# Linear attention and MLP on one core: four more tiles transposed by VectorE, and a new order of query work around the first MLP block

## The chip, the cores and the metric

The kernel runs on one core of a Trainium2 chip. The core has TensorE (PE, the matrix multiplier; PEld is its loading of the stationary operand), VectorE (DVE), ScalarE (ACT), GpSimd (POOL) and SyncE (SP, which here only issues transfers). A transfer is issued in program order on the queue of the engine that issues it (`SPq`, `ACTq`) and carried by 16 DMA engines. The metric is the device time of one execution in microseconds, lower is better.

## The reference

The input x has 2048 rows of 448 columns. Two layers follow one another with the same weights; all is float32.

```
phi = lambda t: where(t > 0, t + 1, exp(t)) + 1e-6
def A(x):                                   # linear attention, 16 heads of 28
    q, k, v = split_heads(x @ wqkv)
    kv  = sum over rows of phi(k)^T v       # per head, 28 x 28
    z   = sum over rows of phi(k)
    o   = (phi(q) @ kv) / (phi(q) . z + 1e-6)
    return merge_heads(o) @ wo
def B(x):                                   # MLP, 1792 wide
    return gelu_tanh(x @ w1 + b1) @ w2 + b2
for layer in range(2):
    x = x + A(layernorm(x))
    x = x + B(layernorm(x))
```

Note that `phi` needs exp of min(t, 0), plus max(t, 0): the kernel computes max(t, 0) + exp(min(t, 0)) and adds the 1e-6 later.

## The kernel before, in words

**Rows and splits.** The 2048 rows are 16 tiles of 128 rows (t = 0 to 15), four to a block. Every factor of a large product is split into a high and a low half (`XH`, `XL`; `w1h`, `w1l`; `gh`, `gl`), and three products high x high, high x low, low x high are added. ScalarE makes the high half by a cast, VectorE the low half by a subtraction. For a product, TensorE needs a tile with its columns on the partitions, so each normalised tile is transposed.

**Two ways to transpose.** `transpose_x` (line 259) has TensorE do it: four transposes into a PSUM bank `tp`, and `split_x` (273) then casts from `tp` and subtracts. A tile's last 64 columns are doubled ahead of it by a ScalarE copy (in `stage_n` for attention, in `o_n`, line 914, for the MLP). The other way leaves TensorE out: `turn` (298) has VectorE transpose 32 x 32 squares within a tile (two instructions, 384 columns and the tail) into `sq`; two tiles share one such buffer of 1024 columns, 512 KB, and `turn_one` (320) fills a buffer of 512 columns, 256 KB, with one tile. `store_sq` (307) writes it to DRAM on SP's queue, `spread` (312) reads it back with four transfers that put the squares in their places, and `split_t` (327) casts and subtracts from what came back, `sp`.

**Stage one of a layer: keys and the sum G.** `phase1` (697) goes through the tiles in steps t. A step is a string of tokens, `STEPS` (640) or the default `STEP`, and each token issues one piece of work on the engines, in that order: `K` is the key product of tile t (`stage_k`), `kp` its phi, `kh` and `kl` its halves, `X` the split of tile t + 1 (`stage_x`, 466), `T` its transposes by TensorE if it takes the first way (`stage_b`, 459), `s` the split of the normalised rows (`stage_s`), `a`, `n` and `v` or `tu` statistics, normalising and turning of later tiles (`stage_a`, `stage_n`, `stage_t`, 448), `sp` the spreads of all that is stored (`stage_sp`), `ld` loads of x, `G` the product of the keys of tile t - 1 with the normalised rows, added up over all tiles, `Q` the query product, `qp` the phi of queries. `bg` loads and splits a piece of the MLP's weights in layer 0 (ScalarE and GpSimd). An odd tile's turn also stores its pair. `TURNED = (8, 0)` (433) says from which tile on a layer takes VectorE's way: tile 8 in layer 0, all tiles in layer 1.

`k_at`, `q_at` and `g_at` (484 and below) give the places of the low products among the eleven matmuls of a product: a later place gives the low half more time.

**From stage one to the MLP.** The string `ORDER` (631) is the same kind of list for what lies between: the last G, the small matrices made of G, then for the first block of four tiles the attention output (`o`), its statistics (`la`, `o_ln`, line 896), normalising (`lb`), turning (`tu`, `turn_xm`, line 928), storing (`st`), spreading (`sp`, transfers in turn on SP's and ScalarE's queue) and splitting (`x`, `m_split`, line 935). Tiles 0 and 1 share a buffer, tile 2 has its own, and tile 3 is transposed by TensorE (`T3`, `m_transpose`, line 924). The query products of tiles 9 to 15 stand between these tokens (`Q`, `Qx`, `Qy`, `Qa`), so that TensorE has work while the block's tiles are got ready. A query's phi is two tokens: `Qi` (`phi_first`, line 576) is two ScalarE passes, Relu of -q and Exp of minus that, and `Qj` (`phi_last`, line 583) is VectorE's max(q, 0) plus that, and its store. Tokens take the queries in the order of their products.

**The MLP.** `mlp1` (961) is the product with a piece of w1, `hp` (its first one takes all high halves of the block first), then GELU on ScalarE, the cast to `gh` on ScalarE and the subtraction to `gl` on VectorE. `mlp2` (981) is the product with w2, added over 14 pieces into `y`. The next block's attention output and splits are issued between these pieces.

**What sets the order.** Nothing is planned by a program: every engine and every queue runs its instructions in the order in which the tokens issue them, and an instruction waits until what it reads is there and its buffer is free. Buffers come from named pools with a few buffers each (tags `"A"`, `"B"`, `"S"`, `"e"`, `"E"`).

## Time and profile before

| | before |
|---|---|
| median of 3 runs (lowest to highest) | 866.67 us (866.61 to 866.70) |
| the profiled execution | 866.77 us |
| its span in the profile | 865.0 us |
| TensorE busy | 859.5 us, 99% |
| VectorE busy | 489.9 us, 57% |
| ScalarE busy | 354.0 us, 41% |
| GpSimd busy | 209.1 us, 24% |

The span runs from the first to the last instruction that the profiler recorded; 1.77 us of the execution lie around it. In the span, layer 0's key products end at 96.8 us, the MLP of its first block begins at 135 us, and layer 1's key products begin at 436 us.

How to read the rows: a row of the timeline has the start, the time (both in us), the engine, the line of the kernel, the operation, the tile written and the tiles read (`psk<-wk,XL`), the shape and the number of instructions that it merges; in brackets stands an idle time before it and what ended it. In a merged row the time is that from its first to its last instruction. A matmul's own duration includes its pipeline, so two starts tell more of its cost than its duration. A row of the waits has who waited, for whom, the total, the number and the mean, in us. `ACTq` and `SPq` are transfers being issued. In a row of the transfers, the last two numbers are the size of one transfer and its time from issue to landing in us.

### The profile page before, as it was taken

To read this page: it belongs to the slowest core of one execution; us is meant where nothing else is said; L and a number is where in the kernel's file an instruction comes from. 1 tells how busy PE (TensorE), PEld (TensorE's weight loads), DVE (VectorE), ACT (ScalarE), POOL (GpSimd) and SP (SyncE) were. 2 spreads that over 40 slices of the span, in tenths; PEclk is the share of its full clock that TensorE was granted. 3 is DMA by queue.
4 is the path that set the end of the run, shared out by engine and by line. 5 is a ranking of instruction groups with operands and counts; after the bars stand their busy time and mean duration, and the time that the engine had idled before them with its cause. 6 is when DMAs were issued, how large, how long until landed. Compare 5 with 4: busy or idle time off the path is not lost.

```text
span 865.0 us, 11671 instructions
## 1 busy us (share of the span) xinstructions
PE 859.5 (99%) x4173; PEld 769.9 (89%) x4173; DVE 489.9 (57%) x956; ACT 354.0 (41%) x634; POOL 209.1 (24%) x242
## 2 busy tenths in 40 slices
PE   9999999999999999999999999999999999999998
PEld 8999988888888888888899998988888888888887
DVE  7888676559455443236477877664674383533112
ACT  6776656333323322333356565632232233223231
POOL 3565612235013012012222343120220140140000
PEclk9999999999999999999999999999999999999999
DMA  5475546633313502051145543362332423111001
GB/s 168 131 241 178 187 112 206 194 112 109 135 60 114 150 0 98 1 182 49 49 149 187 164 129 97 108 217 81 116 107 91 135 74 114 50 49 42 1 1 43
DMA packets 65082, 95.81 MB, mean 111 GB/s; under 512 B 9088, under 2 KB 59904, under 8 KB 65024
## 3 DMA queue, kind: packets, MB, share of 16 engines
q1 hardware_dynamic: 63696, 94.13, 33.8%
q10 hardware_dynamic: 1328, 0.93, 0.4%
q8 instruction: 33, 0.54, 0.3%
q14 instruction: 25, 0.20, 0.1%
HBM read 56.70 MB, written 35.13 MB: 106 GB/s over the span
## 4 chain that ended last, share of the span: by engine, by line
PE 95%; ACT 2%; DMA 1%; DVE 1%; issue 0%; POOL 0%; ACTq 0%; SPq 0%; DVEq 0%
PE hp L972 31%; PE y L1002 10%; PE y L1001 10%; PE y L1003 10%; PE G L622 8%; PE psk L353 8%; PE psq L353 5%; PE op L891 2%; PE op L890 2%; PE op L892 2%; DMA sp<-sq_m 1%; PE op L880 1%; PE op L879 1%; PE op L881 1%; PE kvp L786 1%; PE mp L796 1%
## 5 line engine op out<-in xcount | busy, mean ns | idle before, releaser
L978 DVE TENSOR_TENSOR gl<-g,gh 128x512 fp32r<-128x512 f32 x112 | 83.2, 743 | 293.2 <-ACT gh L977 293.2
L974 ACT ACTIVATE g<-hp,b1s 128x512 f32<-128x512 f32 x112 | 77.1, 688 | 400.1 <-PE hp L972 400.1
L1002 PE MATMUL y<-w2l,gh 128*128 128x448 f32 x447 | 163.6, 366 | 0.0
L1001 PE MATMUL y<-w2h,gh 128*128 128x448 f32 x447 | 162.2, 363 | 0.0
L1003 PE MATMUL y<-w2h,gl 128*128 128x448 f32 x447 | 160.3, 359 | 0.1
L972 PE MATMUL hp<-XH,w1h 128*128 128x512 f32 x336 | 130.7, 389 | 0.0
L972 PE MATMUL hp<-XH,w1l 128*128 128x512 f32 x336 | 130.7, 389 | 0.0
L972 PE MATMUL hp<-XL,w1h 128*128 128x512 f32 x336 | 130.1, 389 | 0.0
L215 POOL TENSOR_TENSOR brs<-bve,mhalf 128x1 f32<-128x1 f32 x55 | 34.8, 632 | 258.4 <-DVE bve L214 257.9
L1001 PEld LDWEIGHTS y<-w2h,gh 128*128 128x128 f32 x447 | 83.7, 187 | 9.8 <-ACT gh L977 0.5
L1002 PEld LDWEIGHTS y<-w2l,gh 128*128 128x128 f32 x447 | 83.9, 188 | 6.9
L1003 PEld LDWEIGHTS y<-w2h,gl 128*128 128x128 f32 x447 | 84.0, 188 | 5.8 <-DVE gl L978 0.9
L972 PEld LDWEIGHTS hp<-XL,w1h 128*128 128x128 f32 x336 | 63.1, 188 | 13.1
L972 PEld LDWEIGHTS hp<-XH,w1h 128*128 128x128 f32 x336 | 63.0, 187 | 10.7
L972 PEld LDWEIGHTS hp<-XH,w1l 128*128 128x128 f32 x336 | 63.1, 188 | 9.9
L977 ACT CAST gh<-g 128x512 fp32r<-128x512 f32 x112 | 69.6, 622 | 3.6
L840 POOL TENSOR_TENSOR pz<-pq,zb 128x448 f32<-128x448 f32 x32 | 37.0, 1162 | 103.3 <-DVE dn L846 67.1
L353 PE MATMUL psk<-wk,XH 128*128 128x448 f32 x210 | 61.8, 364 | 0.0
L353 PE MATMUL psq<-wq,XH 128*128 128x448 f32 x196 | 57.5, 366 | 0.0
L478 POOL TENSOR_TENSOR xnl<-x,xnh 128x384 fp32r<-128x384 f32 x32 | 35.0, 1092 | 69.3 <-ACT xnh L477 56.0
L622 PE MATMUL G<-kh,xnh 128*128 128x448 f32 x128 | 46.8, 368 | 0.0
L336 DVE TENSOR_TENSOR XL<-sp,XH 128x512 fp32r<-128x512 f32 x54 | 45.3, 851 | 2.1 <-ACT XH L335 2.1
(185 smaller groups left out, 1491.1 us busy)
## 6 DMA issues: line engine op xcount, KB each, us to landing
x<-in_A_x_dram SPq DMA_DIRECT2D x32, 224.0 KB, 3.7
pq_d<-eq SPq DMA_DIRECT2D x32, 224.0 KB, 2.7
pq<-pq_d SPq DMA_DIRECT2D x32, 224.0 KB, 3.1
sq_m<-sq SPq DMA_DIRECT2D x14, 512.0 KB, 2.6
x<-x_d SPq DMA_DIRECT2D x32, 224.0 KB, 3.7
sp<-sq_m SPq DMA_DIRECT2D x52, 128.0 KB, 2.8
sq_a<-sq SPq DMA_DIRECT2D x12, 512.0 KB, 2.9
sp<-sq_a SPq DMA_DIRECT2D x48, 128.0 KB, 2.7
```

The source lines that it names most:

```text
L336: eng.tensor_tensor(lo.rearrange("p (c i n) -> p c i n", c=4, n=32), x, f(h), op=OP.subtract)
L353: pe.matmul(o, x, p, start=(i == 0), stop=(i == 10))
L478: pool.tensor_tensor(lo[:, :TL], xn[:, :TL], f(h[:, :TL]), op=OP.subtract)
L622: pe.matmul(acc[c], w, k, start=first and c not in others[0], stop=last and c not in others[1])
L840: pool.tensor_tensor(pz, pqt[l, b * 4 + j], tr.zb, op=OP.mult)
L972: pe.matmul(o, w, r, start=(k == 0), stop=(k == len(made) - 1))
L974: act.activation(g, hp, AF.Gelu_apprx_tanh, bias=b1s[:, i:i + 1])
L977: act.copy(gh, g)
L978: dve.tensor_sub(gl, g, f(gh))
L1001: pe.matmul(acc[j], gh[:, s], w2h[:, i], start=first, stop=False)
L1002: pe.matmul(acc[j], gh[:, s], w2l[:, i], start=False, stop=False)
L1003: pe.matmul(acc[j], gl[:, s], w2h[:, i], start=False, stop=stop)
```

## The change

Five things are changed together:

- In layer 0, tiles 6 and 7 take VectorE's way too (`TURNED` becomes 6). The steps 3 to 11 of layer 0 are written anew: each pair of tiles is turned, stored and spread in other steps than before, and the last pair, tiles 14 and 15, later. The three functions that place the low products follow.
- In most of these steps the split of the next tile (`X`) is issued ahead of the keys' phi (`kp`).
- In both layers the fourth tile of the MLP's first block is turned by VectorE instead of TensorE: `tu3`, `st2` and `sp2` stand where `T3` stood, and its split, `x3`, now comes last of the four.
- For the queries of tiles 12, 13 and 14 the first step of phi is min(q, 0) by VectorE (`Qm`) and one Exp by ScalarE (`Qe`), instead of two passes by ScalarE.
- The two buffers of one tile, for tile 2 and tile 3, come from different pools ("A" and "B").

```diff
--- before.py
+++ after.py
@@ -311,14 +311,14 @@
 
     def spread(key, h, queues=(sp,)):
         d = stored.pop((key, h))
-        r = spreads[key, h] = half("sp") if d.shape[1] == 1024 else t512("A", 2, "sp")
+        r = spreads[key, h] = half("sp") if d.shape[1] == 1024 else t512("AB"[h - 1], 2, "sp")
         d = d.rearrange("(i r) (m f) -> m r i f", i=4, m=4)
         for m in range(4):
             eng = queues[m % len(queues)]
             eng.dma_start(r[m * 32:(m + 1) * 32].rearrange("r (i f) -> r i f", i=4), d[m])
 
-    def turn_one(x, key):
-        sq = squares[key, 1] = t512("A", 2, "sq")
+    def turn_one(x, key, h):
+        sq = squares[key, h] = t512("AB"[h - 1], 2, "sq")
         sq = sq.rearrange("p (m c n) -> p c m n", m=4, c=4, n=32)
         dve.transpose(sq[:, :3], x[:, :TL].rearrange("p (c m n) -> p c m n", c=3, n=32))
         dve.transpose(sq[:, 3].rearrange("p (u m) n -> p u m n", u=2),
@@ -326,7 +326,7 @@
 
     def split_t(key, t, hi, lo, eng=dve):
 
-        x = spreads[key, t // 2]
+        x = spreads[key, t - 1 if (key, 2) in spreads and t == 3 else t // 2]
         if x.shape[1] == 512:
             x = x.rearrange("p (i c n) -> p c i n", i=4, c=4)
         else:
@@ -430,7 +430,7 @@
     sts = {}
 
 
-    TURNED = (8, 0)
+    TURNED = (6, 0)
     tails = {}
 
     def stage_a(l, t):
@@ -483,18 +483,18 @@
 
     def k_at(l, t):
         if t < 9:
-            return (3, 6, 9, 11) if t == 0 or l == 0 and 2 < t < 8 else (2, 5, 8, 11)
+            return (3, 6, 9, 11) if t == 0 or l == 0 and 2 < t < 6 else (2, 5, 8, 11)
         return (2, 5, 8, 11) if t == 9 else (1, 4, 7, 10)
 
     def q_at(l, t):
         if t < 9:
-            return (2, 5, 8, 11) if l == 0 and t < 7 else (2, 4, 7, 10) if t == 0 else (1, 4, 7, 10)
+            return (2, 5, 8, 11) if l == 0 and t < 5 else (2, 4, 7, 10) if t == 0 else (1, 4, 7, 10)
         return {11: (4, 7, 10, 11), 12: (5, 7, 9, 11),
                 13: (5, 8, 10, 11), 15: (1, 5, 8, 11)}.get(t, (1, 4, 7, 10))
 
     def g_at(l, t):
         if t < 9:
-            return (4, 7, 10) if l == 0 and 0 < t < 6 else (3, 6, 9)
+            return (4, 7, 10) if l == 0 and 0 < t < 4 else (3, 6, 9)
         return (2, 5, 8) if t < NT - 1 else (2, 6, 9)
 
     def stage_k(l, t, cs=range(4)):
@@ -579,6 +579,16 @@
         act.activation(e, o, AF.Relu, scale=-1.0)
         act.activation(e, e, AF.Exp, scale=-1.0)
         begun.append((l, t, o, e))
+
+    def phi_min():
+        l, t, o = qo.pop(0)
+        e = t512("e" if t < NT - 2 else "E", 3 if t < NT - 2 else 2, "eq")[:, :D]
+        dve.tensor_scalar(e, o, 0.0, None, op0=OP.min)
+        begun.append((l, t, o, e))
+
+    def phi_exp():
+        e = begun[-1][3]
+        act.activation(e, e, AF.Exp)
 
     def phi_last():
         l, t, o, e = begun.pop(0)
@@ -631,8 +641,8 @@
     ORDER = [
         "Q ld1 ld0 ld2 G qz1 qz0 qz2 gt qs1 Q Qp kv qs0 tq1 Qx mask tq0 qs2 ld3 b "
         "m0 qh1 ql1 m1 ms0 qh0 ql0 m2 ms1 m3 ms2 tq2 ms3 Qi qz3 o0 qh2 qs3 la0 ql2 Qj o1 tq3 qh3 la1 ql3 "
-        "o2 lb0 tu0 la2 o3 lb1 tu1 st0 la3 lb2 tu2 st1 Qy Q lb3 T3 sp0 sp1 Qi Qa x3 Qj x0 x1 x2 Qi Qj pre "
-        "Qa Qi Qj Qa Qi Qj Qi Qj "
+        "o2 lb0 tu0 la2 o3 lb1 tu1 st0 la3 lb2 tu2 st1 Qy Q Qi lb3 tu3 sp0 st2 Qm sp1 Qe Qa sp2 Qj Qj "
+        "Qm Qe Qj x0 x1 x2 pre Qa Qm Qe x3 Qa Qi Qj Qj "
     ] * LAYERS
     DEFER = NT - sum(tok in ("Q", "Qa", "Qy") for tok in ORDER[0].split())
 
@@ -640,12 +650,15 @@
     STEPS = {
         (0, 1): "T X a3 q1 s kh n3 kl q1 G bg ld",
         (0, 2): "K T X s a4 kp n4 a5 kh kl n5 a6 G bg Q ld",
-        (0, 3): "qp K T X s a7 kp kh n6 kl a8 G bg Q ld",
-        (0, 4): "qp K T X s a9 kp kh n7 n8 kl n9 v8 v9 G bg Q ld sp",
-        (0, 8): "qp K T X s a kp n kh kl tu a14 G bg Q ld sp",
-        (0, 9): "qp K T X s kp n14 kh kl v14 G bg",
-        (0, 10): "K T X s a15 kp n15 kh kl v15 G bg sp",
-        (0, 11): "K T X kp s kh kl G bg",
+        (0, 3): "qp K T X n6 s a7 kp kh n7 kl v6 v7 G bg Q ld sp",
+        (0, 4): "qp K T X s a8 kp kh n8 a9 kl v8 n9 G bg Q ld",
+        (0, 5): "qp K s X kp kh v9 a10 kl n10 G bg Q ld sp",
+        (0, 6): "qp K s X v10 kp kh a11 kl n11 G bg Q ld",
+        (0, 7): "qp K s X kp v11 kh a12 kl n12 G bg Q ld sp",
+        (0, 8): "qp K s X kp v12 kh a13 kl n13 a14 G bg Q ld",
+        (0, 9): "qp K X s v13 kp n14 kh kl G sp bg",
+        (0, 10): "K X s v14 kp a15 kh kl n15 G bg",
+        (0, 11): "K X v15 kp s kh kl G sp bg",
         (1, 0): "K T X s kp kh kl a n tu Q ld sp",
     }
     NORM = (
@@ -914,30 +927,17 @@
     def o_n(l, b, j):
         t = b * 4 + j
         xn = xns["m", l, t] = ln_norm(sts.pop(("m", l, t)), f"xm{l}_{t}", OP.add if b == 0 else OP.subtract)
-        if b == 0 and j == 3:
-            act.copy(xn[:, D:], xn[:, TL:D])
 
     def add_bias(l, b, j):
         t = b * 4 + j
         pool.tensor_tensor(xt[l, t], xt[l, t], b2b, op=OP.add)
-
-    def m_transpose(l, b, j):
-        xn = xns.pop(("m", l, b * 4 + j))
-        transpose_x(xn, xn[:, TL:], ("m", l, b), j)
 
     def turn_xm(l, j):
         xn = xns.pop(("m", l, j))
         if j < 2:
             turn(xn, ("m", l, 0), j)
         else:
-            turn_one(xn, ("m", l, 0))
-
-    def m_split(l, b, j):
-
-        if j < 3:
-            split_t(("m", l, b), j, *block(("m", l, b)).pieces(j))
-        else:
-            split_x(("m", l, b), j)
+            turn_one(xn, ("m", l, 0), j - 1)
 
 
     def q_prep(l, b, j, tr):
@@ -1133,15 +1133,14 @@
 
         tok_ = SimpleNamespace(
             Q=lambda j: stage_q(l, fill.pop(0)), Qp=lambda j: fill_qphi(), Qv=lambda j: stage_qphi(j or 9),
-            Qi=lambda j: phi_first(), Qj=lambda j: phi_last(), Qx=lambda j: stage_q(l, fill[0], (0,)),
+            Qi=lambda j: phi_first(), Qm=lambda j: phi_min(), Qe=lambda j: phi_exp(), Qj=lambda j: phi_last(), Qx=lambda j: stage_q(l, fill[0], (0,)),
             Qy=lambda j: stage_q(l, fill.pop(0), (1, 2, 3)),
             Qa=lambda j: stage_q(l, fill.pop(0), tag="acc"), G=lambda j: stage_g(l, NT - 1, acc, lambda: trans_z(tr, zs[l])),
             ld=lambda j: (load_pq(l, 0, j), load_x(l, j)), gt=lambda j: trans_gt(tr, acc),
             kv=lambda j: trans_kv(tr), mask=lambda j: trans_mask(tr), m=lambda j: trans_m(tr, j),
             ms=lambda j: trans_ms(tr, j), qz=lambda j: q_z(l, 0, j, tr), qs=lambda j: q_scale(l, 0, j, tr),
             tq=lambda j: q_transpose(l, 0, j), qh=lambda j: q_high(l, 0, j), ql=lambda j: q_low(l, 0, j), o=lambda j: o_mm(l, 0, j, tr),
-            la=lambda j: o_ln(l, 0, j), lb=lambda j: o_n(l, 0, j), T=lambda j: m_transpose(l, 0, j),
-            x=lambda j: m_split(l, 0, j), tu=lambda j: turn_xm(l, j),
+            la=lambda j: o_ln(l, 0, j), lb=lambda j: o_n(l, 0, j), x=lambda j: m_part(l, 0, j), tu=lambda j: turn_xm(l, j),
             st=lambda j: store_sq(("m", l, 0), j), sp=lambda j: spread(("m", l, 0), j, (sp, act)), pre=pre, b=biases)
         for tok in ORDER[l].split():
             name, j = tok.rstrip("0123456789"), int("0" + tok.lstrip("abcdefghijklmnopqrstuvwxyzQTG"))
```

## The prediction

> **What bounds the kernel now.** I read the page first (busy shares), then the list of waits, then the timeline at the places that the change touches.
>
> ```profile
> span 865.0 us, 11671 instructions
> PE 859.5 (99%) x4173; PEld 769.9 (89%) x4173; DVE 489.9 (57%) x956; ACT 354.0 (41%) x634; POOL 209.1 (24%) x242
> ...
> PE warm L170 <- DVE one L164: 1.1, 1, 1.1
> PE psk L567 <- ACT wk L137: 0.8, 1, 0.8
> ```
>
> TensorE is busy for 99% of the span and waits, as the profile shows it, for 1.9 us. So a matmul taken out of its stream is time won, unless the work put in its place makes TensorE wait; and there is nearly no wait that a faster ScalarE could shorten. The rest is about those two things.
>
> **The change part by part.**
>
> *Transposes taken from TensorE.* These rows are its stream around tile 6's transposes (first four) and around those of the MLP block's fourth tile (last four):
>
> ```profile
> 42.61 0.37 PE L353 MATMUL psk<-wk,XL 128*128 128x448 f32 x1
> 42.81 0.49 PE L264 MATMUL tp<-ident,x 128*128 128x128 f32 x3
> 43.14 0.27 PE L264 MATMUL tp<-ident,b2b 128*128 128x128 f32 x1
> ...
> 43.46 0.36 PE L622 MATMUL G<-kl,xnh 128*128 128x448 f32 x1
> ...
> 127.71 0.37 PE L353 MATMUL psq<-wq,XL 128*128 128x448 f32 x1
> 127.92 0.60 PE L264 MATMUL tp<-ident,xm 128*128 128x128 f32 x4
> 128.28 1.06 PE L353 MATMUL psq<-wq,XH 128*128 128x448 f32 x4
> 129.17 0.36 PE L353 MATMUL psq<-wq,XL 128*128 128x448 f32 x1
> ```
>
> From 42.61 to 43.46 are 0.85 us with two ordinary matmuls in them, which start 0.20 us apart elsewhere: four transposes cost 0.45 us. From 127.71 to 129.17 are 1.46 us with five matmuls: 0.46 us. There are four such groups (tiles 6 and 7, and the fourth tile in each of two layers): 4 x 0.45 = **-1.8 us**. The ScalarE copies that go (two tails in the first stage, the 64-column copy per layer) stood beside waits and are worth nothing.
>
> *The fourth tile's new way.* Before, its transposed copy was split ahead of the others while the other three tiles' DMA round trip ran. After, the tile itself makes that trip: two transposes on VectorE, a 256 KB store on SP, four 64 KB reads on SP and ScalarE's queue, then the cast on ScalarE. The first matmul of the MLP reads the high halves of all four tiles, so it cannot start before that cast. Its cover is the three query tiles (13 to 15) that TensorE works on; it used up:
>
> ```profile
> 125.33 0.58 DVE L323 STREAM_TRANSPOSE sq<-xm 128x384 f32<-128x384 f32 x1
> 125.83 0.27 DVE L324 STREAM_TRANSPOSE sq<-xm 128x128 f32<-128x128 f32 x1
> 126.95 0.51 DVE L227 TENSOR_SCALAR xm<-x,bst,brs 128x448 f32<-128x448 f32 x1 [0.85 <-POOL brs L908]
> ...
> 127.56 1.77 ACTq L318 DMA_DIRECT2D sp<-sq_m  x4
> ...
> 131.37 1.66 ACT L335 CAST XH<-sp 128x512 fp32r<-128x512 f32 x3 [0.36 <-DMA sp<-sq_m]
> 131.64 0.61 DVE L585 SCALAR_TENSOR_TENSOR eq<-psq,eq 128x448 f32<-128x448 f32 x1
> 132.18 1.89 DVE L336 TENSOR_TENSOR XL<-sp,XH 128x512 fp32r<-128x512 f32 x3
> ...
> 127.92 3.29 DMA sp<-sq_m
> ...
> 136.63 0.58 ACT L580 ACTIVATE eq<-eq 128x448 f32<-128x448 f32 x1
> 139.98 0.69 DVE L978 TENSOR_TENSOR gl<-g,gh 128x512 fp32r<-128x512 f32 x1 [2.12 <-ACT gh L977]
> ...
> 135.01 0.39 PE L972 MATMUL hp<-XH,w1h 128*128 128x512 f32 x1
> 140.00 0.47 PE L1001 MATMUL y<-w2h,gh 128*128 128x448 f32 x1
> 140.31 0.37 PE L1002 MATMUL y<-w2l,gh 128*128 128x448 f32 x1
> 140.73 0.47 PE L1003 MATMUL y<-w2h,gl 128*128 128x448 f32 x1
> 141.04 0.36 PE L1001 MATMUL y<-w2h,gh 128*128 128x448 f32 x1
> ```
>
> I follow it in the times of this profile. The tile is normalised at 127.47; its two transposes take 0.77 us as tile 2's do (125.33 to 126.10): 128.25. The store goes out on SP at 128.3, ahead of the second spread there. A 256 KB store alone and the transfers issued at that moment took
>
> ```profile
> sq_m<-sq SPq DMA_DIRECT2D x1, 256.0 KB, 2.2
> ...
> sp<-sq_m ACTq DMA_DIRECT2D x2, 64.0 KB, 3.3
> ```
>
> so it lands between 130.5 and 131.6. I take 131.6, as the 16 DMA engines are full then (four spreads of 128 KB are under way, and the row at 127.92 took 3.29 us). ScalarE's queue must now issue its two reads of it, in order ahead of the next exponentials: the first waits for the store, the second also for the first spread's last transfer, whose semaphore it reuses (landed at 131.21). At 0.44 us an issue (1.77 / 4) ScalarE is free at 131.65 at the earliest, 132.7 at the latest, and I take **132.2**.
>
> From there ScalarE and VectorE take turns, in the order that the program has. Exponential of tile 13's query to 132.8; VectorE's last pass of it (0.54 to the next row) to 133.35; three low halves (0.60 each; the high halves run ahead of them) to 135.15; then VectorE's new min(q, 0) of tile 14's query, for which no row exists: the nearest, a one-input pass over 448 columns at 0.51 and a pass reading the same PSUM tile at 0.61, bound it, and I take 0.55 to 135.7. The exponential behind it waits for that min, and the fourth tile's cast stands behind the exponential: 0.49 to the cast's start, 0.62 for the cast: 136.9. TensorE wants to start at 135.01 - 0.45 = 134.56, so **it waits 2.35 us** in each layer (1.8 to 2.9 from the ends above). The min saves ScalarE a pass of about the exponential's length for each of three queries, but puts VectorE's queue, with three low halves in it, ahead of the cast.
>
> A part of this comes back. Before, TensorE's first y matmuls wait for the first gh and gl: their starts stand 0.31, 0.42 and 0.31 us apart instead of 0.20, so 0.44 us are lost, because ScalarE has four query exponentials and the table load still to do. After, one query is left behind the cast: its exponential starts some 0.6 us after the cast, and from the last exponential to the end of the first gl are 4.04 us (136.63 to 140.67): 4.6 us, while TensorE gets there only 4.99 us after the cast (135.01 to 140.00). So -0.44. With the transposes' 0.45 a layer pays 2.35 - 0.45 - 0.44 = +1.46 us. Layer 1 has the same rows 425.3 us later.
>
> *Tiles 6 and 7 in the first stage.* Each pair now needs a store and a spread, and all later pairs are stored one step later (13 in step 9, 15 in step 11). Two places are tight, tile 6's trip and the last pair's:
>
> ```profile
> 34.50 0.61 DVE L533 TENSOR_TENSOR za<-psk,za 128x448 f32<-128x448 f32 x1
> 50.51 0.36 PE L622 MATMUL G<-kl,xnh 128*128 128x448 f32 x1
> ...
> 80.08 0.32 SPq L310 DMA_DIRECT2D sq_a<-sq  x1
> 87.37 0.62 ACT L335 CAST XH<-sp 128x512 fp32r<-128x512 f32 x1 [0.88 <-DMA sp<-sq_a]
> 88.02 0.69 DVE L336 TENSOR_TENSOR XL<-sp,XH 128x512 fp32r<-128x512 f32 x1 [0.79 <-ACT XH L335]
> 89.97 0.37 PE L353 MATMUL psk<-wk,XL 128*128 128x448 f32 x1
> ```
>
> Store to cast is 7.3 us, and tile 14's cast already waits 0.88 us for it; the low half is done at 88.71, 1.26 us before TensorE reads it. After, TensorE is 0.9 us earlier there, and tile 15 is turned only behind the low half of tile 12, whose own trip began at about 71.5: 71.5 + 7.3 + 0.62 + 0.69 + 0.7 = 80.75 instead of 80.05. So the slack of 1.26 becomes 1.26 - 0.9 - 0.7 = -0.3 us. Tile 6: its pair is turned behind the row at 34.50 (0.4 us later than there, then 2 x 0.77), so stored at 37.0; with three loads between store and spread on SP the trip takes nearer 8 us, and the cast, at 45, now stands ahead of key 5's exponentials. Cast 0.6, two exponentials 1.1, the keys' pass 0.6, one tile's transposes 0.8, statistics 0.9 and kl 0.6 end at 49.6, just when TensorE, 0.9 earlier than 50.51, reads kl. I put **+0.4 us** on both together; between 0 (if VectorE is a little ahead) and 1.4 (if both trips are 0.5 us longer).
>
> Here a rule bears on the size:
>
> ```profile
> 63.25 0.69 DVE L336 TENSOR_TENSOR XL<-sp,XH 128x512 fp32r<-128x512 f32 x1
> 69.91 1.50 DVE L336 TENSOR_TENSOR XL<-sp,XH 128x512 fp32r<-128x512 f32 x1
> 69.70 1.15 POOL L404 TENSOR_TENSOR w1x<-stg,w1x 64x448 fp32r<-64x448 f32 x1
> ```
>
> A low half made from a spread takes 0.69 us, or 1.50 us while GpSimd works; tiles 6 and 7 now are of this kind. I count 0.69, because GpSimd's split of tile 5 should be over when tile 6 gets there. The Trainium skill (SBUF — State Buffer, "Who interferes with whom") says that a VectorE instruction with two SBUF inputs and a GpSimd instruction that reads SBUF exclude each other; the row agrees (+0.8 us), and by it the sum would be up to 0.8 us higher if they met.
>
> The shifted positions of low products, the splits ahead of the keys' phi, and the earlier loads of the next queries have a microsecond or more of cover each in the queues of ScalarE, VectorE and SP, and I count nothing for them.
>
> **The sum.** Transposes -1.8, waits for the fourth tile 2 x 2.35 = +4.7, y's waits 2 x -0.44 = -0.9, first stage +0.4: **+2.4 us**. The profiled execution took 866.77 us (span 865.0 and 1.77 around it), 0.1 above the median of 866.67, so I forecast **869.1 us**. Its own ends: per layer +0.9 to +2.0, first stage 0 to +1.4 with its two groups' -0.9: 867.6 to 871.2.
>
> **The rivals.**
> *The cover holds (faster).* If the fourth tile's cast is done by 134.5, in both layers, TensorE never waits for it, all 1.8 us stay, and y's waits go too: 866.67 - 1.8 - 0.9 = 864.0, with nothing lost in the first stage. For it: the query work covers 6.3 us from 128.25. Against: store and spread alone take 2.2 + 2.8 us, and the orders on ScalarE and VectorE put a min, an exponential and three splits between. It decides where the wait is under 1.14 us a layer: 2 x (1.14 - 0.89) = 0.5 = 0.9 - 0.4, and the kernel is not slower.
> *Only the trip counts (same).* If ScalarE's issue does not block as I think, the cast follows the landing, at 134.6 and 0.6 on: a wait of 0.7 us a layer, 2 x (0.7 - 0.89) - 0.9 + 0.4 = -0.9: 865.8.
> *TensorE's clock falls.* The granted clock is full in all slices of the page, but the first products run at half speed:
>
> ```profile
> PEclk9999999999999999999999999999999999999999
> ...
> 1.12 4.21 PE L170 MATMUL warm<-one 128*128 128x128 f32 x18 [1.12 <-DVE one L164]
> ```
>
> 18 products in 4.0 us are 0.22 us each, against 0.11 for the transposes at 42.81. If a pause of 2.35 us threw the clock back, 4.0 us at half speed would lose 2 us a layer: 869.1 + 4 = 873.1. No pause of this length is in the trace. The Trainium skill (TensorE: Matmul & The Clock Gate, Part 1) has the clock halve after an idle window of about 3.4 us, free-running; by it 2.35 us would hardly do, and no run here shows it.
>
> **How the numbers follow.** Forecast 0.74, cover holds 0.05, only the trip 0.13, clock 0.08. A 0.2% step is 1.7 us (864.9, 868.4), about what a measurement tells from none. The forecast's own spread puts 0.56 above 868.4 and 0.18 between. Slower: 0.56 + 0.08 = 0.64; same: 0.18 + 0.13 = 0.31; faster: 0.05. Leaving out cover, trip's lower part and clock, the range is 866.4 to 871.2.
>
> **What would show it.** After: no transposes from tile 6 on; a TensorE wait of about 2.4 us for XH ahead of the first hp in both layers, with ScalarE's cast last in order behind min and exponential; y's first matmuls 0.20 apart; a few tenths at the keys of tile 14. Wrong, if that wait is under 1 us, if the store lands before 130.7, or if keys of tiles 12 to 15 wait over a microsecond.

## The result, and the profile after

The changed kernel takes **875.8 us** (median of four, 874.75 to 876.81) against 866.68 us: a ratio of 1.0104 (95% interval 1.009 to 1.0117). It is 9.1 us slower. I had forecast +2.4 us and a range that ended at 871.2.

The page of the profiled execution (875.2 us, span 873.4 us), and under it the waits in which TensorE takes part (who waited, for whom: total, times, longest, in us):

```profile
span 873.4 us, 11687 instructions
PE 860.3 (99%) x4157; PEld 768.8 (88%) x4157; DVE 496.8 (57%) x970; ACT 349.7 (40%) x624; POOL 210.7 (24%) x242
...
PE hp L972 <- ACT XH L335: 5.9, 2, 3.0
PE psk L353 <- DVE XL L336: 1.5, 2, 0.9
...
PE G L632 <- DVE kl L526: 0.5, 1, 0.5
```

TensorE has 16 instructions fewer, as meant, and is busy for *more* time. Three kinds of wait of 0.5 us and more that did not exist before stand here. They sum to 7.9 us, less than the 8.4 by which the span grew, though 1.8 us of transposes went out of it. So some of the time is elsewhere. The starts of landmark matmuls in the two traces tell where (us; each difference is that of the stage between two landmarks):

| from | to | before | after | difference |
|---|---|---|---|---|
| start of the span | first key product | 7.07 | 6.58 | -0.5 |
| first key product | first matmul on G's blocks (stage one of layer 0) | 98.77 | 101.21 | +2.4 |
| there | first hp, layer 0 | 29.17 | 31.91 | +2.7 |
| there | first key product of layer 1 (MLP) | 301.03 | 302.34 | +1.3 |
| there | first matmul on G's blocks, layer 1 | 95.13 | 95.13 | 0.0 |
| there | first hp, layer 1 | 29.17 | 31.76 | +2.6 |
| there | end | 304.70 | 304.46 | -0.2 |

The sum is +8.3. It is made up of the two transitions, stage one, and something in the MLP of layer 0 that layer 1 does not have. That last is seen in TensorE's timeline around the first hp of both layers:

```profile
136.31 0.36 PE L353 MATMUL psq<-wq,XL 128*128 128x448 f32 x1
139.69 0.49 PE L972 MATMUL hp<-XH,w1h 128*128 128x512 f32 x1 [3.03 <-ACT XH L335]
140.03 0.39 PE L972 MATMUL hp<-XH,w1l 128*128 128x512 f32 x1
140.26 0.40 PE L972 MATMUL hp<-XH,w1h 128*128 128x512 f32 x1
...
143.01 0.63 PE L972 MATMUL hp<-XL,w1x 128*128 128x512 f32 x1
143.44 0.63 PE L972 MATMUL hp<-XH,w1h 128*128 128x512 f32 x1
143.87 0.63 PE L972 MATMUL hp<-XH,w1l 128*128 128x512 f32 x1
...
565.71 0.36 PE L353 MATMUL psq<-wq,XL 128*128 128x448 f32 x1
568.92 0.50 PE L972 MATMUL hp<-XH,w1h 128*128 128x512 f32 x1 [2.85 <-ACT XH L335]
```

An ordinary query matmul is followed by the next 0.20 us later; here hp follows after 3.38 and 3.21 us, so TensorE loses **3.18 and 3.01 us** ahead of the first hp. Then hp's matmuls stand 0.23 us apart (140.03 to 140.26), and from 141 us on 0.43 us apart (143.01 to 143.44). The table of stretches shows why. A row has the stretch, its length, the busy time of PE, PEld, DVE, ACT and POOL, the granted TensorE clock (1.00 is full), the busy share of the DMA engines and GB/s:

```profile
136.50:139.70 3.20, 0.17 (x2) 0.01 (x1) 2.05 (x5) 1.72 (x5) 0.00 (x0) 1.00 0.96 324
139.70:141.00 1.30, 1.30 (x6) 1.09 (x7) 1.30 (x3) 1.25 (x3) 1.29 (x1) 1.00 0.85 167
141.00:144.30 3.30, 3.30 (x10) 2.52 (x9) 0.43 (x1) 1.82 (x3) 0.39 (x1) 0.50 0.96 339
144.30:148.00 3.70, 3.70 (x18) 3.24 (x17) 0.69 (x1) 2.00 (x4) 0.00 (x0) 0.98 0.75 251
```

For 3.3 us the clock is granted at 0.50: 1.7 us lost. It falls 1.3 us *after* TensorE has gone on. In layer 1 of this execution it does not fall at all. The mean granted clocks of the four executions are 0.998, 0.995, 0.996 and 0.997, and one such interval is 3.4 x 0.5 / 873 = 0.002 of the mean: one to two or so of them in each.

Why hp waits is on ScalarE, VectorE and in the chain of waits. The rows below are the spread's issues on ScalarE's queue with the exponentials (L591) and casts (L335) behind them, VectorE's rows of the same time, and the chain's piece for the fourth tile's store:

```profile
134.06 0.85 ACTq L318 DMA_DIRECT2D sp<-sq_m  x2
134.95 0.58 ACT L591 ACTIVATE eq<-eq 128x448 f32<-128x448 f32 x1 [3.38 <-DMA sq_m<-sq]
135.44 1.64 ACT L335 CAST XH<-sp 128x512 fp32r<-128x512 f32 x3
138.56 0.58 ACT L591 ACTIVATE eq<-eq 128x448 f32<-128x448 f32 x1 [1.48 <-DVE eq L586]
139.04 0.60 ACT L335 CAST XH<-sp 128x512 fp32r<-128x512 f32 x1
...
136.10 1.89 DVE L336 TENSOR_TENSOR XL<-sp,XH 128x512 fp32r<-128x512 f32 x3
137.91 0.62 DVE L586 TENSOR_SCALAR eq<-psq 128x448 f32<-128x448 f32 x1
...
130.22 3.75 DMA sq_m<-sq
```

ScalarE stands idle for 3.38 us for the fourth tile's store. Then comes the order that the forecast described, piece for piece: exponential, casts and low halves, the min at 137.91 behind them, ScalarE's 1.48 us of waiting for it, the exponential, the cast, hp.

In stage one TensorE stalls at three places, ahead of the low key half of tile 5 and ahead of the low halves of tiles 10 and 14:

```profile
49.10 0.36 PE L632 MATMUL G<-kh,xnh 128*128 128x448 f32 x1
49.99 0.47 PE L632 MATMUL G<-kl,xnh 128*128 128x448 f32 x1 [0.52 <-DVE kl L526]
...
71.70 0.37 PE L632 MATMUL G<-kl,xnh 128*128 128x448 f32 x1
72.93 0.47 PE L353 MATMUL psk<-wk,XL 128*128 128x448 f32 x1 [0.87 <-DVE XL L336]
...
90.80 0.36 PE L632 MATMUL G<-kl,xnh 128*128 128x448 f32 x1
91.79 0.47 PE L353 MATMUL psk<-wk,XL 128*128 128x448 f32 x1 [0.62 <-DVE XL L336]
```

By their starts, less 0.20 each: 0.7, 1.0 and 0.8 us. The chain of waits from 45 to 92 us is one ring that goes round four times (start, time, what):

```profile
57.55 0.63 ACT XH L335
...
58.21 1.54 DVE XL L336
...
60.29 0.47 DVE sq L303
...
60.98 3.19 DMA sq_a<-sq
...
65.56 5.87 DMA sp<-sq_a
...
71.53 0.63 ACT XH L335
...
72.88 0.49 DVE sq L303
...
73.58 2.58 DMA sq_a<-sq
...
77.50 3.01 DMA sp<-sq_a
```

The split of tile 8 (57.55), behind it on VectorE the turn of tile 11 (60.29), the pair's store (60.98) and spread, the split of tile 10 (71.53), behind it the turn of tile 13, its store and spread, and so on to tile 14 at 90.39. A pair is turned only after the split that waited for the pair before it. Before, pairs were stored every 12 us (at 55.86, 68.11 and 80.08), which is TensorE's pace; a round of the ring takes 14.0 us (57.55 to 71.53) where the spread is slow. Before, tile 10's spread had landed 5.5 us ahead of its cast (63.71 and 69.24). Now its pair is stored 5.1 us later, and from the store to the last landing are 10.4 us, not 7.9, so that this slack is gone; why that spread is the slowest of the five is not shown.

### The profile page after: what moved, and what is told of

Same layout as the page of the kernel before. It is cut to its first block, busy times and chain, and to the rows that moved or that the text cites. A ratio compares the mean times of both kernels' runs of the same rounds, so it can differ in the third digit from the quotient of the medians.

```text
span 873.4 us, 11687 instructions
## 1 busy us (share of the span) xinstructions
PE 860.3 (99%) x4157; PEld 768.8 (88%) x4157; DVE 496.8 (57%) x970; ACT 349.7 (40%) x624; POOL 210.7 (24%) x242
## 4 chain that ended last, share of the span: by engine, by line
PE 87%; DMA 6%; DVE 3%; ACT 1%; issue 1%; SPq 1%; POOL 1%; DVEq 0%; ACTq 0%; POOLq 0%
PE hp L972 32%; PE y L1002 10%; PE y L1001 10%; PE y L1003 10%; PE G L632 5%; PE psk L353 5%; PE psq L353 3%; DMA sp<-sq_a 2%; PE op L904 2%; DMA sq_a<-sq 2%; PE op L903 2%; PE op L905 2%; DMA sq_m<-sq 1%; SPq L318 1%; PE op L893 1%
## 5 line engine op out<-in xcount | busy, mean ns | idle before, releaser
L336 DVE TENSOR_TENSOR XL<-sp,XH 128x512 fp32r<-128x512 f32 x58 | 48.4, 846 | 9.5 <-ACT XH L335 9.5
L632 PE MATMUL G<-kl,xnh 128*128 128x448 f32 x128 | 46.2, 366 | 0.5 <-DVE kl L526 0.5
```

The source lines that it names most:

```text
L336: eng.tensor_tensor(lo.rearrange("p (c i n) -> p c i n", c=4, n=32), x, f(h), op=OP.subtract)
L632: pe.matmul(acc[c], w, k, start=first and c not in others[0], stop=last and c not in others[1])
```

## The experiments

All of them compute the whole result. Waits are given by the starts of matmuls, less 0.20 us, as above.

**The two halves of the change, each alone.** First, everything behind stage one as changed, with `TURNED`, `STEPS` and the low products' places as before:

```diff
-    TURNED = (6, 0)
+    TURNED = (8, 0)
...
 (STEPS, k_at, q_at and g_at as before the change)
```

> Layer 0's stage one as before (transposes of tiles 6 and 7 by TensorE, the old steps), all that comes after it as changed. Theory (now, from the trace after the change): the fourth tile's trip makes TensorE wait 3.2 us ahead of the first hp in each layer, +0.1 behind it, -0.45 for the transposes, -0.44 for y's waits: 2 x 2.4 = +4.8 us, 871.5 us; and each such pause can throw TensorE's clock to half speed for some microseconds, which costs another 0 to 4 us and differs between executions (spread over 1 us). Rival (the forecast's own sum): 2 x 1.46 = +2.9 us, 869.6 us, with the clock at 1.000 and the runs within 0.3 us of each other.

Measured: 872.95 us (872.43 to 874.78), ratio 1.0078 (1.0061 to 1.0094). The waits ahead of hp are 2.97 and 2.90 us. Half-speed matmuls follow in layer 0 of the profiled execution and not in layer 1; the four granted clocks are 0.998, 0.995, 1.000 and 0.997, and the spans follow them: 870.8, 873.1, 870.0 and 870.9 us. The forecast's own sum (869.6) does not hold; the transition alone is the greater part of the loss, and the part that differs between executions goes with the clock.

Second, stage one alone (the new `STEPS`, `TURNED = (6, 0)`, the old `ORDER`):

> Tiles 6 and 7 by VectorE with the new steps of layer 0's stage one; all that comes after as before. Theory: three stalls of TensorE in stage one (0.8 at the keys of tile 5, 1.1 at tile 12's split, 0.9 at tile 14's, 0.3 of small ones) less 0.9 for eight transposes: +2.2 us, 868.9 us. The clock stays at 1.000 and the runs lie within 0.3 us, since no pause is over 1.3 us. Rival (the forecast): +0.4 - 0.9 = -0.5, 866.2 us. Rival for the clock: if it fell for another reason than the pause, it falls here too.

Measured: 869.35 us (868.78 to 870.19), ratio 1.0032 (1.0019 to 1.0045). Stalls of 0.8, 0.6 and 1.3 us at the three places, and the granted clock 0.999 to 1.000 in every execution: pauses of up to 1.3 us leave it alone. (What the expectation calls tile 12's split is tile 10's: the pair stored at 61 us is tiles 10 and 11.) The two parts sum to 6.3 + 2.7 = 9.0 us, the whole to 9.1: as far as executions that differ by 2 us can tell, they do not help or hinder each other.

**The order ahead of the fourth tile's cast.**

```diff
-        "Qm Qe Qj x0 x1 x2 pre Qa Qm Qe x3 Qa Qi Qj Qj "
+        "Qm Qe Qj x0 x1 x2 pre Qa x3 Qm Qe Qa Qi Qj Qj "
```

> The changed kernel with the fourth tile's split issued ahead of tile 14's min and exponential. Theory (the order on ScalarE and VectorE costs what the trip does not): the cast starts right behind the three others, so the wait ahead of the first hp falls from 3.2 to about 1.2 us in each layer, and the clock does not fall; but the two last queries' exponentials then lie between it and the first GELU, so y waits 0.5 to 1.0 us a layer. Sum against the changed kernel without its lost clock (873.5): -4.0 + 1.0 to 2.0: 870.5 to 871.5 us, runs within 0.3 us. Rival (only the landing of the tile counts): the wait stays above 2.5 us, and the time at 873 or above.

Measured: 870.87 us (869.79 to 873.71), ratio 1.0055 (1.0034 to 1.0075). The waits ahead of hp fall to 1.4 and 0.8 us, and no half-speed matmul follows. As expected, part of it comes back ahead of y: 0.8 us, and 0.4 more among its first matmuls, in each layer. The last expectation failed: executions differ by 3.9 us at a clock of 0.999 to 1.000. The profiled one (the slowest) waits 1.2 us at 47 us, in stage one, where the changed kernel's trace has no wait: two of the four spreads of tiles 6 and 7 landed at 47.0 and 47.6 us, where all had landed by 45.4 in the changed kernel's trace, and the other two came at 44.4 and 44.7. The cast waited for them:

```profile
46.99 0.36 PE L353 MATMUL psq<-wq,XH 128*128 128x448 f32 x1
48.40 0.47 PE L353 MATMUL psk<-wk,XH 128*128 128x448 f32 x1 [1.05 <-ACT XH L335]
```

So the new stage one has places without slack, where a late transfer moves the total. That the other executions differ for the same reason is not shown, as they were not profiled.

**The min, undone.** The queries' first step by two ScalarE passes (`Qi`) again, nothing else:

```diff
-  ... sp0 st2 Qm sp1 Qe Qa sp2 Qj Qj Qm Qe Qj x0 x1 x2 pre Qa Qm Qe x3 ...
+  ... sp0 st2 sp1 Qi Qa sp2 Qj Qj Qi Qj x0 x1 x2 pre Qa Qi x3 ...
```

> The changed kernel with the queries' exponentials made by two passes of ScalarE as before, instead of VectorE's min and one pass. If the min behind the three low halves is what holds the fourth tile's cast, ScalarE goes on from its third cast at once: two passes for tile 14 (1.1 us) in place of waiting 1.5 us and one pass (0.5), but one pass more for tile 13 (0.55): the wait ahead of hp falls by 0.2 to 0.4 us a layer. If ScalarE's load were the bound, it would rise by 0.5 to 1.1.

Measured, in one execution: 875.03 us. The waits are 2.77 and 2.50 us instead of 3.18 and 3.01: 0.4 and 0.5 us less, a little over what was expected. One pass *more* on ScalarE for each of three queries makes the wait *shorter*. Behind both pauses the clock fell (granted mean 0.995), so that nothing of it is seen in the time.

**ScalarE's queue freed of the wait for the store.** From the kernel with the transition alone changed, the fourth tile's four reads all go out on SP:

```diff
- spread(("m", l, 0), j, (sp, act))
+ spread(("m", l, 0), j, (sp,) if j == 2 else (sp, act))
```

> As the run with the transition alone changed, but the four reads of the fourth tile go out on SP's queue alone, so that ScalarE has no issue to wait for. Theory (ScalarE stands 3.4 us behind an issue that waits for the store, and everything behind it is late): tile 13's exponential and the three casts run some 2 us earlier, the fourth tile's cast follows its landing (0.6 us later than there, four issues in a row on SP), and the wait ahead of the first hp falls from 2.9 to between 1.3 and 1.8 us a layer; 869.1 + 1.77 - 2 x 1.3 = 868.3 us, without a fall of the clock. Rival (only the landing counts): the wait does not fall, since the landing is later: 871 us or more.

Measured: 868.19 us (867.65 to 869.85, ten executions), ratio 1.0019 (1.001 to 1.0029), 4.8 us less than the 872.95 without this line. The waits are 1.79 and 1.28 us, the clock 0.999 to 1.000. ScalarE's rows ahead of hp, and hp:

```profile
133.17 0.62 ACT L335 CAST XH<-sp 128x512 fp32r<-128x512 f32 x1 [0.62 <-DMA sp<-sq_m]
135.08 0.58 ACT L591 ACTIVATE eq<-eq 128x448 f32<-128x448 f32 x1 [1.29 <-DVE eq L586]
135.56 0.60 ACT L335 CAST XH<-sp 128x512 fp32r<-128x512 f32 x1
...
136.22 0.50 PE L969 MATMUL hp<-XH,w1h 128*128 128x512 f32 x1 [1.63 <-ACT XH L335]
```

The reads had landed at 135.33 us, so this is nearly the trip alone, and the trip alone is already 1.3 to 1.8 us late. The transposes (0.45) and y's waits (0.44) give back 0.9 a layer: issued in this way, the fourth tile's trip does not pay. With the reads on two queues (the run with the transition alone) they had landed 2.8 us behind the store, here 3.3. By an estimate from these two, a trip with two free queues would wait 0.5 us less in each layer, and would be about even; no run has it.

**The turns a step earlier.** Stage one alone again, with each pair from tile 9 on turned in the step in which it is normalised:

```diff
-        (0, 4): "qp K T X s a8 kp kh n8 a9 kl v8 n9 G bg Q ld",
-        (0, 5): "qp K s X kp kh v9 a10 kl n10 G bg Q ld sp",
+        (0, 4): "qp K T X s a8 kp kh n8 a9 kl v8 n9 v9 G bg Q ld sp",
+        (0, 5): "qp K s X kp kh a10 kl n10 v10 G bg Q ld",
...
-        (0, 10): "K X s v14 kp a15 kh kl n15 G bg",
-        (0, 11): "K X v15 kp s kh kl G sp bg",
+        (0, 10): "K X s a15 kp n15 kh kl v15 G bg sp",
+        (0, 11): "K X kp s kh kl G bg",
```

> As the run with stage one alone changed (tiles 6 and 7 by VectorE), but each pair from tile 9 on is turned, stored and spread a step earlier, as before the change, instead of behind the split of an earlier tile. Theory (the stalls at tiles 12 and 14 come from a ring: a pair is turned behind the split that waits for the pair before it): the stalls at 72 and 91 us (0.6 and 1.3 there) vanish, the one at tile 5's keys (0.8) stays: +0.8 + 0.3 - 0.9 = +0.2, 866.8 us. Rival (the DMA engines are too full for one more pair): stalls of over 1 us in sum remain at 72 and 91 us, 868 us or more.

Measured: 867.42 us (866.82 to 870.77, ten executions), ratio 1.0012 (1.0003 to 1.0022), 1.9 us less than with the turns behind the splits. The one at 870.77 has a granted clock of 0.998, the others 0.999 to 1.000; it was not profiled, so its pauses are not known. The stall at tile 14 is gone, and so is that at tile 5's keys, which I had expected to stay. One of 1.0 us stays at 72 us (and 0.2 us at 60), but now for another reason, as its rows on TensorE, ScalarE and VectorE show:

```profile
72.52 0.48 PE L353 MATMUL psk<-wk,XL 128*128 128x448 f32 x1 [0.79 <-DVE XL L336]
...
69.25 0.60 ACT L335 CAST XH<-sp 128x512 fp32r<-128x512 f32 x1
...
71.79 0.68 DVE L336 TENSOR_TENSOR XL<-sp,XH 128x512 fp32r<-128x512 f32 x1
```

The cast is early; the low half comes 1.9 us behind it, because VectorE has a normalising, a turn, statistics and a query's pass to do first. In a window of 8 us (64 to 72) it is busy for 7.8 us. So without the ring tile 10's cast comes 2.1 us earlier (69.25 for 71.31 in the run with stage one alone), tile 14's stall is gone, and what is left at 72 us is VectorE's fill. The stall at tile 5's keys need not have been the ring's: the same edit takes tile 9's turn out from ahead of those keys' low half on VectorE, where it took 0.7 us (47.97 to 48.66) of that run's stall of 0.8. Neither expectation was met in full: 866.8 by the ring alone, 868 or more by the DMA engines.

**The min alone.** From the kernel before, min and one exponential for the queries of tiles 11 to 13, the fourth tile still by TensorE:

```diff
- ... T3 sp0 sp1 Qi Qa x3 Qj x0 x1 x2 Qi Qj pre Qa Qi Qj Qa Qi Qj Qi Qj
+ ... T3 sp0 Qm sp1 Qe Qa x3 Qj x0 x1 x2 Qm Qe Qj pre Qa Qm Qe Qj Qa Qi Qj Qi Qj
```

> The kernel before, with VectorE's min and one exponential for the queries of tiles 11, 12 and 13, and nothing else changed (the fourth tile by TensorE). Theory: ScalarE comes 1.5 us earlier to the first GELU, so y's first matmuls no longer wait: 2 x -0.44 = -0.9, 865.8 us. Rival: the min puts VectorE's queue ahead of the splits, and a wait of 0.3 us or more a layer comes in ahead of hp: 866.7 us or above.

Measured: 872.03 us (869.98 to 873.19), ratio 1.0058 (1.0043 to 1.0073). The theory was wrong, and the rival was right about the side but not about the place. hp starts on time, but y waits 2.1 us in each layer, and behind that pause too the clock falls in some executions (0.998 in three, 1.000 in one). ScalarE's rows, and TensorE's first y:

```profile
134.60 0.58 ACT L591 ACTIVATE eq<-eq 128x448 f32<-128x448 f32 x1 [1.46 <-DVE eq L586]
136.40 0.58 ACT L591 ACTIVATE eq<-eq 128x448 f32<-128x448 f32 x1 [1.22 <-DVE eq L586]
...
141.86 0.47 PE L1011 MATMUL y<-w2h,gh 128*128 128x448 f32 x1 [1.87 <-ACT gh L987]
```

With two ScalarE passes a query followed the one before it after 1.05 us (the kernel before: 134.54, 135.59, 136.63). With the min the next exponential comes after 1.80 us: VectorE does min, ScalarE the exponential, VectorE the last pass, and only behind that the min of the next query. ScalarE saves a pass of 0.53 for each and waits 1.2 to 1.5 for two of the three; the first, at 129.20, does not wait for its min.

**The pause by itself.** From the kernel before, the third tile's split is held back behind the queries of tiles 11 to 14 and some ScalarE passes on one column that do nothing, first 3, then 14 of them:

```diff
- ... x3 Qj x0 x1 x2 Qi Qj pre Qa Qi Qj Qa Qi Qj Qi Qj
+ ... x3 Qj x0 x1 Qi Qj pre Qa Qi Qj Qa Qi Qj (3 or 14 idle passes) x2 Qi Qj
```

> The kernel before, where the third tile's split of the MLP's first block is held back behind the queries of tiles 11 to 14 and three short ScalarE passes, to make TensorE pause ahead of the first hp for about 2.2 us in each layer (near the 2.35 us forecast), with all other work as before. It measures the clock by itself. If a pause trips the clock only from 2.5 us on (the shortest seen to do it), no half-speed matmuls follow: 866.7 + 2 x (2.2 - 0.44) = 870.2 us, runs within 0.5 us. If pauses of 2.2 us do it at times, runs differ by 1.7 us steps, and up to 3.5 us come on top.

Measured: 869.59 us (869.39 to 870.87), ratio 1.0037 (1.0023 to 1.0051). The pauses are 2.1 and 1.4 us; four of five executions have a clock of 0.999 to 1.000, and one 0.997, which is also the longest (span 869.1 against 867.7 to 868.3).

> As the run with the short pause (1.4 and 2.1 us there), with eleven more short ScalarE passes ahead of the third tile's split: TensorE pauses about 2.2 us longer, some 3.6 and 4.3 us. Theory (a pause can put TensorE's clock at half speed for about 3.4 us, surely so when it is this long): half-speed matmuls behind the pause in both layers in each execution, 1.7 us each: 867.7 + 1.77 + 2 x 2.2 + 2 x 1.7 = 877.3 us, clock 0.995 to 0.996, runs within 0.5 us of each other. Rival (the clock falls for another reason, at random): as often as with the short pause, 873.9 us in most runs.

Measured: 877.45 us (877.10 to 877.77), ratio 1.0124 (1.011 to 1.0138). The pauses are 4.5 and 3.8 us; behind both, half-speed matmuls, and a granted clock of 0.996 in each of the four executions, which lie within 0.7 us. Two rows of TensorE's clock, as above:

```profile
134.90:139.50 4.60, 0.34 (x2) 0.00 (x0) 1.25 (x2) 4.16 (x19) 1.13 (x1) 0.95 0.84 226
139.50:142.50 3.00, 2.96 (x7) 2.38 (x8) 1.32 (x2) 2.50 (x4) 0.00 (x0) 0.51 0.90 299
```

Here the clock falls within the pause already (0.95 over 4.6 us is 0.46 us at half speed), and 2.9 us behind it: 3.4 us in all again. The rival, a fall at random, does not hold.

**Towards a faster version.** One min only, issued ahead of the last pass of the query before it, so that ScalarE need not wait:

```diff
-        "Qa Qi Qj Qa Qi Qj Qi Qj "
+        "Qa Qi Qm Qj Qe Qa Qi Qj Qj "
```

> The kernel before, with VectorE's min for the query of tile 14 alone, issued ahead of tile 13's last pass. Theory (in the run with three mins each min stood behind the last pass of the query before it, so ScalarE waited 1.2 to 1.5 us for each to save a pass of 0.53): with the min issued early ScalarE does not wait, saves one pass, and reaches the first GELU 0.4 us earlier: y's waits fall from 0.44 to about 0.05 us a layer, 866.7 - 0.8 = 865.9 us. Rival (any min on VectorE delays): 866.7 us or more.

Measured: 866.24 us (865.82 to 866.53, eleven executions), ratio 0.9994 (0.9985 to 1.0003): less than the measurement can tell from no change. In the profiled execution y's waits are 0.1 us in layer 1 and still 0.5 in layer 0, so what was expected came in one layer of two. A min issued so is no loss.

The same with tiles 6 and 7 by VectorE, early turns, and the keys' low products later in each product (places 5, 8, 10, 11); tile 14's statistics one step later, tile 15's turn ahead of the keys' halves:

> The one early min, and stage one with tiles 6 and 7 by VectorE with the early turns, tile 14's statistics a step later and the low products of the keys later in each product. Theory (the stalls at 60 and 72 us came from low halves late by 0.3 and 1.0 us on a full VectorE; low products 0.6 us later and one statistic less in that step take most of them): stalls of 0 to 0.5 us in sum, 865.9 - 0.9 + 0 to 0.5 = 865.0 to 865.5 us, faster than the kernel before. Rival (VectorE has no room in that stretch): the stalls move and stay at 1 us, 866 us or above.

Measured: 868.49 us (867.71 to 869.44, eleven executions), ratio 1.0022 (1.0013 to 1.0031), as the rival had it. The stalls at 60 and 72 us are gone, and 2.1 us of new ones stand between 74 and 82 us, where keys' halves wait behind what was put ahead of them. With those pieces behind the keys' passes instead:

```diff
-        (0, 9): "qp K X s a14 kp kh kl n14 v14 G bg",
-        (0, 10): "K X s a15 kp n15 v15 kh kl G bg sp",
+        (0, 9): "qp K X s kp a14 kh kl n14 v14 G bg",
+        (0, 10): "K X s kp a15 kh kl n15 v15 G bg sp",
```

> As the run with the one early min and tiles 6 and 7 by VectorE, but the statistics of tiles 14 and 15 behind the keys' last pass, and tile 15's normalising and turn behind the keys' low half. Theory (the 2.1 us of stalls at 74 to 82 us there came from these pieces standing on VectorE ahead of the keys' passes): those stalls vanish, 0.3 to 0.6 us stay at tile 5's keys, and the last pair, stored 1 us later, costs 0 to 0.5 at 91 us: 866.6 - 0.9 - 0.4 + 0.3 to 1.1 = 865.6 to 866.4 us. Rival (VectorE has no room for two more tiles in this stretch whatever the order): over 1.5 us of stalls stay in sum, 866.8 us or more.

Measured: 866.91 us (866.47 to 868.66, eleven executions), ratio 1.0005 (0.9996 to 1.0015): no difference. The stalls sum to 1.4 us still (0.6 the longest, at a low half at 82 us). Each of the two reorderings moved them by a step: in the orders tried, VectorE's queue had no place for two more tiles in this stretch that cost nothing, and the 0.9 us of transposes paid for that and no more. None of these versions is measurably faster than the kernel before.

## Why the prediction was wrong

The direction was right, and no step of the mechanism in the transition was missing; the size was not: +2.4 was forecast, +9.1 measured, outside the range. In the profiled execution the span grew by 8.3 us, 5.9 more than forecast: stage one makes 2.9 of it, layer 0's MLP with its fallen clock 1.8, the two waits ahead of hp 1.5, layer 1's MLP 0.2, and the time to the first key product, which the change does not touch, takes back 0.5. So three steps failed: stage one's +0.4, the store's size, and the clock set apart from the sum.

- *Transposes, -0.45 us for each group.* Right: hp's wait in the layers is 3.18 and 3.01, and the stage up to it grew by 2.73 and 2.58.
- *The wait for the fourth tile, 2.35 us.* Right in kind, too small in size: 3.18 and 3.01. The store went out at 130.22 and landed at 133.98, after 3.75 us; I had taken 3.3, the upper of two rows. ScalarE was free 0.9 us behind that landing and not 0.6; by the sum's own 0.44 an issue, two issues behind the landing at 131.6 end at 132.5, and I had put 132.2. These two make the missing 0.8; everything behind it (three low halves, min, exponential, cast) took within 0.1 us what the sum had for it. What failed here is the size of the store among eight reads, with the 16 DMA engines busy for 0.84 of its time. Neither row that bounded it had both its bytes and its crowd: the 64 KB reads of 3.3 us had the crowd (0.80 from 128.3 to 131.6) and a quarter of the bytes, the 256 KB store of 2.2 us had the bytes and half the crowd (0.47 from 126 to 128.3).
- *y's waits, -0.44.* Right: y's first matmuls stand 0.20 us apart in both layers. In layer 1, where the clock stayed up, the MLP gained 0.2 us and not 0.44, in part because hp's second matmul now stands 0.11 us late behind the first.
- *Stage one, +0.4 us.* This is the step that failed most: the three stalls are 2.5 us, with the short delays behind them 3.1. I followed tile 6's trip and the last pair's, each from the times of the old trace, and did not follow the pairs between. The two places that I followed, with +0.4 for both together, cost 0.7 and 0.8: each was nearly without slack in the sum itself (tile 6's cast came at 45.45 for 45, and the keys' low half ended at 49.93 for 49.6). (For tile 15's store the sum's terms give 80.81, not 80.75, which changes nothing.) Between them the new steps put each turn behind the split that waits for the pair before, and so a delay is handed on from pair to pair. Tile 10's stall, the largest, was not looked at. For the trip I had 7.3 us from store to cast, one row of four; to their last landing the four trips of the old trace take 7.1 to 8.1, and in the ring the longest was 10.6 to the cast (60.98 to 71.53). The rule on VectorE and GpSimd that the forecast weighed (The Trainium skill, "SBUF — State Buffer", "Who interferes with whom") has its case in the trace: the low half of tile 8 (58.21) took 1.54 us, while GpSimd worked from 57.02 to 59.93. But that is 0.8 us of a round of 14.
- *The clock.* A rival, to which I gave 0.08, as no pause of that length was in the trace. It was part of what happened in every execution of the changed kernel. The price named for it (2 us a layer for 4.0 us at half speed) was near: 1.7 us for 3.4. I had set it apart from the forecast although the forecast's own pause of 2.35 us could bring it: pauses of 2.1 us (before hp, and before y in the run with three mins) did so in some executions. Which of the changed kernel's two pauses does so is chance, as the last section shows.
- *The cover, and the trip alone.* Neither holds. The trip alone would have cost 0.7 us by that rival; the run with the reads on SP shows 1.3 to 1.8.
- *The splits ahead of the keys' phi, counted at nothing.* Not tested by itself, and neither is the change of pools; both stay open.
- *The min, 0.55 us.* It took 0.58 to 0.62. That it puts VectorE's queue into ScalarE's way was said of one query; the run with the min alone shows it for two of its three.

## What to carry to other kernels

A transfer that replaces TensorE's work has to be priced as a chain on the queues as they are at that moment: which issue waits for it, on whose queue, and what stands behind that issue; moving two issues from ScalarE's queue to SP's was worth 2.4 us a layer here, its clock included, five times the fourth tile's transposes. Moving a pass from a busier engine to a freer one is no gain if work then goes to and fro between the two for each item: one pass less made each item 0.75 us longer. And where an engine at 99% is made to pause, count beside the pause what its clock loses behind it; up to 1.8 us nothing was lost in the profiles here, from 2.1 us on 1.7 us at times, from 3.8 us on always. Gaps that lie close together add up in this, as the next section shows.

## What the runs showed of the hardware

The granted clock after a pause of TensorE, over all the runs' profiled executions (one pause a layer):

| pause, us | half-speed matmuls behind it |
|---|---|
| 0.8, 1.3, 1.4, 1.4, 1.8 | in none |
| 2.1 (three) | in one |
| 2.5, 2.8 | in both |
| 2.9, 3.0, 3.0, 3.2 | in two of four |
| 3.8, 4.5 | in both |

Each fall lasted 3.4 us and cost 1.7 us. Behind pauses of 2.1 to 3.2 us it began between 0.3 us before and 1.8 us after TensorE had gone on, and in one kernel with two like pauses (3.18 and 3.01 us) it came behind one and not behind the other. That fits a clock that is decided at the ends of intervals which do not begin with the pause.

The traces show these intervals. They keep the granted clock as stretches with a start and a length, and in all 14 profiled executions every stretch but the last has a length that is a whole multiple of 3.413 us (3.41, 133.12, 136.53, 426.67, 730.45, 860.16 and others). Where the first one begins, between 4.0 and 7.3 us, differs from execution to execution. These are the intervals at the two pauses of the changed kernel, with the columns as above:

```profile
137.61:141.02 3.41, 1.32 (x6) 1.11 (x7) 2.26 (x5) 2.41 (x5) 1.31 (x1) 1.00 0.90 245
141.02:144.43 3.41, 3.41 (x10) 2.63 (x9) 0.41 (x1) 1.90 (x4) 0.37 (x1) 0.50 0.97 341
...
564.27:567.68 3.41, 1.79 (x9) 1.33 (x8) 2.89 (x5) 2.04 (x4) 0.00 (x0) 1.00 0.90 287
567.68:571.10 3.42, 2.18 (x10) 1.80 (x11) 1.83 (x4) 3.27 (x5) 1.16 (x1) 1.00 0.83 272
```

In layer 0, TensorE is busy for only 1.32 us of one interval, and at its end the clock falls. In layer 1 the end of an interval, at 567.68, cuts the pause into two pieces of 1.6 and 1.2 us, and the clock stays. I counted every interval at full clock from 20 to 850 us in the 14 executions, some 3400, by the starts of matmuls (0.20 us for one of 448 columns, 0.23 for 512). The clock fell behind seven of them, in which TensorE had nothing to do for 2.03 to 3.41 us; in all others it had nothing to do for 1.90 us at most. So it is not the length of a pause that decides here, but how much of it lies in one interval, together with the other gaps in it: in the run with three mins, 1.6 us of the 2.1 us pause and 0.4 us among y's first matmuls made up the 2.03. By an estimate from these figures, a lone pause below 1.9 us never costs a fall, one above 4.1 us always does (wherever it is cut, one interval has 2.03 us of it), and between them it is chance.

The Trainium skill (TensorE: Matmul & The Clock Gate, Part 1) has such a window, free-running and 3.4 us long, and says that the clock falls after an idle window of that length. The length agrees with the intervals measured here; that a whole window must be idle does not, as 2.03 us of 3.41 were enough.
